# A linear-attention and Fourier-mixing kernel: batch 0 of the attention in a written order with own tiles, and the last bit of the weights added as an integer

## The chip, the cores and the metric

The kernel runs on one core of a Trainium2 chip. The metric is the device time of one launch in microseconds (us). A core has TensorE (PE; its weight loads are listed as PEld), VectorE (DVE), ScalarE (ACT), GpSimd (POOL) and SyncE (SP), which here only issues DMAs. Each engine works through its own list of instructions in order and waits on semaphores.

## The reference

```python
B, H, S, D = 4, 8, 768, 48
f = 1 / (1 + exp(-f_logit))
for t in range(S):                                   # attention, per batch and head
    state = f[t][:, None] * state + outer(k[t], v[t])
    y[t]  = q[t] @ state
x = y, heads side by side                            # [4, 768, 384]
u = x + real(fft over d (fft over s (x)))            # Fourier mixing
un = (u - mean) / sqrt(var + 1e-6)
out = u + relu(un @ w_ch1) @ w_ch2                   # 384 -> 1536 -> 384
```

The two weight matrices arrive as 64-bit numbers; the kernel turns each into 32-bit floats itself.

## The kernel before, in words

A **unit** is one batch and one pair of heads: 16 units, four to a batch. Queries, keys and forget logs of a unit arrive with the tokens along the free axis, in one tile `qkf` of [128, 3, 768] (heads at partitions 0 to 47 and 64 to 111; between them lie constants), and there are three such tiles. `attention` (L154 to L197) and `outputs` (L318 to L378) are Python generators; each `yield` ends a step.

- Step 1: DVE clamps the logs (L164), ACT makes `g = ln(1 + exp(-f))` (L165, L166), DVE takes running sums per chunk of 128 tokens (L169 to L171), ACT makes `W = exp(g)` (L173), `exp(-g)` (L174) and chunk decays (L176), POOL multiplies `W` by the keys (L178), DVE multiplies the queries (L179).
- Step 2: PE makes the scores (L188, 48 matmuls), DVE copies them under the causal mask into `at` (L192).
- `outputs`: PE turns the keys (L328), ACT copies them (L330), PE makes the state increments (L335, L341), DVE scans them into states (L344); then PE makes `y` from scores and values (L356) and from states (L361), ACT copies it out (L366, L367); then PE turns it back (L372), ACT writes it to the batch's tile `x` (L373), and SP issues the loads of unit u + 3 into the tiles that this unit leaves (L104 for `qkf`, L106 for `v`).

When four units have written a batch's `x`, the generator `fnet` runs on it: sums and differences (L397 to L403), the transform over tokens (`z`, L422), over channels (`mix`, L435), mean and variance (L453 to L458), and for each half of the tokens normalising and turning (L466 to L470), the up projection in 12 blocks (`up`, L479, relu on ACT L482) and the down projection (`po`, L492), sum (L494) and store (L382, L384). Two `x` tiles exist, so batch 2's units write theirs once batch 0 is stored.

**Weights.** The first `fnet` fetches and converts the weights in 24 pieces of [128, 384], twelve of `w1` ahead of the up blocks that use them and twelve of `w2` in the first down projection. `single` (L123 to L146) does one: a 384 KB load into `raw` (two buffers, L128), ACT takes the size (L136), DVE shifts and joins bits of the high word (L138, L139), zeroes what is too small (L141), takes the power of two (L142) and shifts the low word (L140), ACT scales that (L144), POOL multiplies it by the power of two (L145) and adds it to the result (L146). Its temporaries `size`, `pow2` and `tail` share the 14 buffers of `h1`, which also hold the twelve relu outputs of a half.

**Order.** `run` steps all active units once per tick, starts a unit at each tick in batch 0 and at every second tick later (`STEP`), and steps `fnet` twice per tick (`BESIDE`). That order is a priority only: a list scheduler, with cost estimates of its own, fills each engine's list when the program is built, and may put an instruction ahead of earlier ones that it takes to be waiting. After all of it a check decides whether a second, slower form of attention must run; it didn't in these executions.

Of the kernel before, what the change touches and what calls it, by code (L numbers as in the profile page):

```python
# [14 lines left out]
STEP = 2  # L15
BESIDE = 2
# [3 lines left out]
X_MIN = -24.0  # L20
# [3 lines left out]
def kernel(  # L24
# [13 lines left out]
    nc = tc.nc  # L38
    B, HP, _, D, _, S = qkf.shape
    NCH = S // C  # L40
    DM = HP * 2 * D
# [4 lines left out]
    HD = DM // 2  # L46
    R = 64 + D
    ROWS = [slice(64 * r, 64 * r + D) for r in range(2)]
# [13 lines left out]
    def fixed(shape, tag):  # L62
        return const.tile(shape, F32, tag=tag, name=tag)
# [3 lines left out]
    qkf_t = [fixed([128, 3, S], f"qkf{i}") for i in range(3)]  # L67
# [6 lines left out]
    xc = fixed([128, 4, 256], "xc")  # L74
# [25 lines left out]
    def load_unit(u):  # L100
        b, hp = divmod(u, HP)
        t = qkf_t[u % 3]
        for r in (1, 0):
            nc.sync.dma_start(out=t[ROWS[r]], in_=qkf[b, hp, r])  # L104
        vt = p3.tile([128, NCH, 2 * D], F32, tag="v", name=f"v{u}")
        nc.sync.dma_start(out=vt, in_=v[b, hp])  # L106
        return vt

    v_of = {0: load_unit(0)}
    nc.sync.dma_start(out=masks, in_=sel)  # L110
    nc.sync.dma_start(out=ident, in_=ident_in)
    v_of[1] = load_unit(1)
    v_of[2] = load_unit(2)
    nc.sync.dma_start(out=tab, in_=seq_tab)
    nc.sync.dma_start(out=cd[:, :, 0:DM], in_=dim_tab)
    nc.gpsimd.memset(eps, 1e-6)
    for t in at_t + te_t:
        nc.gpsimd.memset(t, 0.0)
    nc.gpsimd.memset(xc[:, :, HD + 1:], 0.0)
    nc.gpsimd.memset(xs[:, :, 0:1], 0.0)  # L120
    nc.gpsimd.tensor_copy(cd[:, :, DM:DM + 1], cd[:, :, 0:1])

    def single(dst, src):  # L123


        n = dst.shape[-1]
        raw = pr.tile([128, n, 2], U32, tag="raw", name="raw")
        nc.sync.dma_start(out=raw.rearrange("p n w -> p (n w)"), in_=src)  # L128
        lo, hi = raw[:, :, 0], raw[:, :, 1]
        size = ph1.tile([128, n], F32, tag="h1", name="size")  # L130
        pow2 = ph1.tile([128, n], F32, tag="h1", name="pow2")
        tail = ph1.tile([128, n], F32, tag="h1", name="tail")
        bits, pow2b, tailb = (t.bitcast(U32) for t in (dst, pow2, tail))
        vec = nc.vector

        nc.scalar.activation(size, hi.bitcast(F32), AF.Abs)  # L136

        vec.tensor_scalar(bits, hi, 3, 0x3FFFFFF8, ALU.logical_shift_left, ALU.bitwise_and)  # L138
        vec.scalar_tensor_tensor(bits, hi, 0xC0000000, bits, ALU.bitwise_and, ALU.bitwise_or)  # L139
        vec.tensor_scalar(tailb, lo, 1, None, ALU.logical_shift_right)  # L140
        vec.scalar_tensor_tensor(dst, size, SMALLEST, dst, ALU.is_ge, ALU.mult)  # L141
        vec.tensor_scalar(pow2b, bits, 0xFF800000, None, ALU.bitwise_and)  # L142

        nc.scalar.activation(tail, tailb, AF.Copy, scale=2.0 ** -51)  # L144
        nc.gpsimd.tensor_tensor(tail, tail, pow2, ALU.mult)  # L145
        nc.gpsimd.tensor_tensor(dst, dst, tail, ALU.add)  # L146
# [7 lines left out]
    def attention(u, x_all):  # L154
# [4 lines left out]
        t = qkf_t[u % 3]  # L159
        Q, K, g = t[:R, 0], t[:R, 1], t[:R, 2]  # L160
        AT = at_t[u % 2]
        W = p2.tile([128, S], F32, tag="W", name=f"W{u}")[:R]
        at = lambda a, i, c: a.rearrange("p (c t) -> p c t", t=C)[:, c, i]
        nc.vector.tensor_scalar(g, g, X_MIN, None, ALU.max)  # L164
# [7 lines left out]
        nc.gpsimd.tensor_copy(T[:, NCH - 1:], g[:, S - 1:S])  # L172
        nc.scalar.activation(W, g, AF.Exp)  # L173
# [4 lines left out]
        nc.gpsimd.tensor_tensor(W, W, K, ALU.mult)  # L178
        nc.vector.tensor_tensor(Q, Q, g, ALU.mult)  # L179
        yield  # L180
# [18 lines left out]
    def attention_by_blocks(u, x_all):  # L199
# [5 lines left out]
        t = qkf_t[u % 3]  # L205
        Q, K, g = t[:R, 0], t[:R, 1], t[:R, 2]
# [18 lines left out]
        w = p1.tile([128, 3, S], F32, tag="eo", name=f"w{u}")[:R]  # L225
        wq, wk, gk = w[:, 0], w[:, 1], w[:, 2]
# [28 lines left out]
        tl = p2.tile([128, S // LEAF], F32, tag="tl", name=f"tl{u}")[:R]  # L255
# [59 lines left out]
        yield  # L315
        yield from outputs(u, x_all, AT, Q, K, None, T)

    def outputs(u, x_all, AT, Q, K, te, T=None):  # L318
# [11 lines left out]
        nc.scalar.copy(kT, ps[:, :(NCH - 1) * 128].rearrange("p (c k) -> p c k", k=128)[:, :, :R])  # L330
        ps = ps_a.tile([128, 2, 512], F32, tag="sc", name=f"ds{u}")
# [22 lines left out]
        for c in range(NCH):  # L354
            for r in range(2):
                nc.tensor.matmul(y[FILL[r], c * C:(c + 1) * C],  # L356
                                 lhsT=vt[:, c, r * D:r * D + (64 if r == 0 else D)], rhs=AT[:, r, c],
                                 start=(c % 4 == 0), stop=(c == 0), skip_group_check=True)
        for c in range(1, NCH):
            for r in range(2):  # L360
                nc.tensor.matmul(y[ROWS[r], c * C:(c + 1) * C], lhsT=st[ROWS[r], :, c - 1],  # L361
                                 rhs=Q[ROWS[r], c * C:(c + 1) * C], start=False, stop=True,
                                 skip_group_check=True)
# [3 lines left out]
        nc.scalar.copy(yT[:, HS + 1:], y[:R, S - 1:HS:-1])  # L367
        yield
# [7 lines left out]
        if u + 3 < B * HP:  # L376
            v_of[u + 3] = load_unit(u + 3)
        yield  # L378
# [121 lines left out]
    def run(unit_of, step, first):  # L500
        left, xs_of, active, behind, done = [HP] * B, {}, [], [], set()
        u = tick = 0
        while u < B * HP or active or behind:
            if u < B * HP and (u < 3 or u - 3 in done) and (first and u < HP or tick % step == 0):
                b, hp = divmod(u, HP)
                if hp == 0:
                    xs_of[b] = p2.tile([128, NCH, DM], F32, tag="x", name=f"x{b}")
                active.append((u, unit_of(u, xs_of[b])))
                u += 1
            for i, unit in list(active):  # L510
                if next(unit, active) is active:
                    active.remove((i, unit))
                    done.add(i)
                    b = i // HP
                    left[b] -= 1
                    if not left[b]:
                        behind.append(fnet(b, xs_of.pop(b), first and b == 0))
            for _ in range(BESIDE):
                while behind and next(behind[0], active) is active:
                    behind.pop(0)  # L520
            tick += 1

    run(attention, STEP, True)


# [8 lines left out]
    with tc.If(again > 0):  # L534
        v_of.update({i: load_unit(i) for i in range(3)})
        run(attention_by_blocks, 3, False)
# [69 lines left out]
```

## Time and profile before

| | |
|---|---|
| median of 3 runs | 709.93 us (708.13 to 710.97) |
| the profiled execution | 707.84 us, of which the instructions' span is 706.0 us |
| busy: PE, DVE, ACT, POOL | 599.4, 247.1, 182.3, 138.7 us |
| mean DMA rate | 50 GB/s over the span |

A busy PE is one with a matmul in its pipeline, not one at full clock: the granted clock is a row of its own. A group's row gives output, inputs, shape and count, then busy time and mean duration; behind the bar stands the idle time ahead of the group and what ended it.

### The profile page before, as it was taken

The numbers are of one execution on the slowest core, as the hardware profiler recorded it, in microseconds if no ns is written. First come the engines' busy times: TensorE is split into PE (matmuls) and PEld (weight loads), VectorE is DVE, ScalarE is ACT, GpSimd is POOL, SyncE is SP. The second block draws the span as 40 slices with busy tenths as digits, with TensorE's granted clock in tenths as the row PEclk, the third lists the DMA queues.
The fourth block names the chain that finished last, engine by engine and source line by source line (L and its number), as shares of the span: only waits on it lengthen the run. The fifth ranks groups of instructions, "written<-read, shape, count | busy, mean of one in ns | idle before, by whom it ended". The sixth has DMA issues, their size and how long they took to land.

```text
span 706.0 us, 8313 instructions
## 1 busy us (share of the span) xinstructions
PE 599.4 (85%) x3458; PEld 371.0 (53%) x3458; DVE 247.1 (35%) x398; ACT 182.3 (26%) x341; POOL 138.7 (20%) x130
## 2 busy tenths in 40 slices
PE   0777898775765799997999999978999997999995
PEld 0656656443432355565656665645555563555552
DVE  3767786885577500039403110152000005000000
ACT  1555454434233121034411320212102101210200
POOL 4231541465455400112300101020000010000001
PEclk9997899988786799998999999997999999899999
DMA  9595553534323100033003000000000000000000
GB/s 167 168 180 100 116 113 68 135 85 95 90 85 96 65 11 1 22 78 70 0 1 73 11 1 23 13 1 0 1 22 13 0 33 1 0 12 22 0 12 27
DMA packets 11182, 35.56 MB, mean 50 GB/s; under 512 B 1600, under 2 KB 3776, under 8 KB 9472
## 3 DMA queue, kind: packets, MB, share of 16 engines
q1 hardware_dynamic: 10368, 32.58, 20.0%
q0 software_dynamic: 768, 2.36, 0.9%
q8 instruction: 29, 0.48, 0.3%
q14 instruction: 17, 0.14, 0.1%
HBM read 30.22 MB, written 4.72 MB: 49 GB/s over the span
## 4 chain that ended last, share of the span: by engine, by line
PE 67%; DVE 15%; POOL 8%; issue 4%; ACT 4%; DMA 2%; POOLq 0%; ACTq 0%; DVEq 0%
PE up L479 27%; PE po L492 24%; POOL tail L145 3%; POOL w L146 3%; PE z L422 3%; PE mix L435 3%; DVE at L192 2%; DVE w L141 2%; DVE qkf L170 2%; PE y L356 2%; PE sc L188 2%; DVE pow L142 2%; PE ds L335 1%; DMA qkf<-in_qkf_dram 1%; PE pt L469 1%
## 5 line engine op out<-in xcount | busy, mean ns | idle before, releaser
L479 PE MATMUL up<-unT,w 128*128 128x384 f32 x576 | 205.8, 518 | 22.6 <-POOL w L146 19.8
L492 PE MATMUL po<-w,h 128*128 128x384 f32 x576 | 198.0, 502 | 16.7 <-POOL w L146 16.7
L479 PEld LDWEIGHTS up<-unT,w 128*128 128x128 f32 x576 | 114.1, 202 | 105.8 <-POOL w L146 23.0
L492 PEld LDWEIGHTS po<-w,h 128*128 128x128 f32 x576 | 110.7, 195 | 100.8 <-POOL w L146 25.8
L494 DVE TENSOR_TENSOR x<-po,x 128x384 f32<-128x384 f32 x24 | 13.4, 558 | 294.5 <-PE po L492 294.4
L482 ACT ACTIVATE h<-up 128x384 f32<-128x384 f32 x96 | 47.1, 491 | 150.4 <-PE up L479 150.4
L384 POOL DMA_INDIRECT out_dram<-x,place x12 | 11.9, 990 | 323.8 <-DVE x L494 317.1
L188 PE MATMUL sc<-qkf,W 48*64 48x128 f32 x768 | 35.7, 313 | 26.9 <-DVE qkf L179 25.5
L192 DVE COPY_PREDICATED at<-causal,sc 128x768 f32<-128x768 uint32 x32 | 32.5, 1032 | 38.0 <-PE sc L188 38.0
L188 PEld LDWEIGHTS sc<-qkf,W 48*64 48x64 f32 x768 | 28.4, 155 | 31.9 <-POOL W L178 21.2
L145 POOL TENSOR_TENSOR tail<-tail,pow 128x384 f32<-128x384 f32 x24 | 32.6, 1360 | 48.4 <-DVE pow L142 47.8
L178 POOL TENSOR_TENSOR W<-W,qkf 112x768 f32<-112x768 f32 x16 | 31.0, 1937 | 25.7 <-ACT W L173 24.9
L356 PE MATMUL y<-at,v 128*64 128x128 f32 (+1 forms) x384 | 33.3, 310 | 1.9 <-ACT yT L367 1.3
L146 POOL TENSOR_TENSOR w<-w,tail 128x384 f32<-128x384 f32 x24 | 31.5, 1311 | 1.8
L356 PEld LDWEIGHTS y<-at,v 128*64 128x64 f32 (+1 forms) x384 | 25.4, 147 | 9.3 <-issue 5.5
L170 DVE TENSOR_TENSOR_SCAN qkf<-qkf,bound 112x768 f32<-112x768 f32 x16 | 28.1, 1755 | 0.4
L172 POOL COPY deep<-qkf 112x1 f32<-112x1 f32 x16 | 3.3, 205 | 125.9 <-DVE qkf L170 118.3
L344 DVE TENSOR_TENSOR_SCAN stt<-ds,te 112x288 f32<-112x288 f32 x16 | 12.1, 754 | 44.0 <-PE ds L341 44.0
L470 ACT COPY unT<-pt 128x384 f32<-128x384 f32 x24 | 11.1, 478 | 61.8 <-PE pt L469 61.8
L435 PE MATMUL mix<-cd,zz 128*128 128x385 f32 x72 | 25.7, 497 | 1.3 <-DVE row L443 1.3
L469 PE MATMUL pt<-ident,un 128*128 128x128 f32 x72 | 13.7, 323 | 14.9 <-DVE mv L454 9.9
L361 PE MATMUL y<-qkf,stt 48*48 48x128 f32 x320 | 22.7, 288 | 4.2 <-DVE stt L344 4.1
(80 smaller groups left out, 526.8 us busy)
## 6 DMA issues: line engine op xcount, KB each, us to landing
qkf<-in_qkf_dram SPq DMA_DIRECT2D x32, 432.0 KB, 6.7
raw<-in_w_ch_dram SPq DMA_DIRECT2D x24, 384.0 KB, 3.1
v<-in_v_dram SPq DMA_DIRECT2D x16, 288.0 KB, 3.3
out_dram<-x SPq DMA_DIRECT2D x12, 192.0 KB, 1.9
tab<-in_seq_tab_dram SPq DMA_DIRECT2D x1, 1158.0 KB, 18.3
cd<-in_dim_tab_dram SPq DMA_DIRECT2D x1, 576.0 KB, 17.1
out_dram<-x,place POOLq DMA_INDIRECT x12, 2.6
masks<-in_sel_dram SPq DMA_DIRECT2D x1, 64.0 KB, 4.9
```

The costliest lines, as they stand in the source:

```text
L145: nc.gpsimd.tensor_tensor(tail, tail, pow2, ALU.mult)
L146: nc.gpsimd.tensor_tensor(dst, dst, tail, ALU.add)
L170: nc.vector.tensor_tensor_scan(g, g, bound[:R], 0.0, ALU.add, ALU.min)
L178: nc.gpsimd.tensor_tensor(W, W, K, ALU.mult)
L188: nc.tensor.matmul(ps[64 * s:64 * s + 64, r, i * C:(i + 1) * C], lhsT=W[ROWS[r], o + 64 * s:o + 64 * s + 64], rhs=Q[ROWS[r], o:o + C], sta ...
L192: nc.vector.copy_predicated(AT[:, :, half], causal.bitcast(U32).unsqueeze(1).unsqueeze(1).to_broadcast([128, 2, NCH // 2, C]), ps[:, :, :N ...
L356: nc.tensor.matmul(y[FILL[r], c * C:(c + 1) * C], lhsT=vt[:, c, r * D:r * D + (64 if r == 0 else D)], rhs=AT[:, r, c], start=(c % 4 == 0), ...
L361: nc.tensor.matmul(y[ROWS[r], c * C:(c + 1) * C], lhsT=st[ROWS[r], :, c - 1], rhs=Q[ROWS[r], c * C:(c + 1) * C], start=False, stop=True, s ...
L435: nc.tensor.matmul(mix[:rows.stop - rows.start, :n], lhsT=zz[:, T, rows], rhs=cd[:, T, :n], start=(T == 0), stop=(T == terms - 1))
L479: nc.tensor.matmul(pp[:, :3 * 128], lhsT=w1[:, kt, m * 128:(m + 1) * 128], rhs=unT[:, kt], start=(kt == 0), stop=(kt == 2))
L482: nc.scalar.activation(h, pp[:, :3 * 128], AF.Relu)
L492: nc.tensor.matmul(po[:, :DM], lhsT=h1[m][:, i * 128:(i + 1) * 128], rhs=w2[:, m], start=(m == 0), stop=(m == NF - 1))
```

## The change: a written order for batch 0, own tiles, and an integer bit

- **Tiles.** `qkf` is split into three `g`, three `k` and four `q` tiles. `load(u, names)` fetches any of logs ("f"), keys, queries and values of a unit, two DMAs for each of the first three. Logs and keys of unit u + 3 are fetched after its W and Q products, queries and values of u + 4 after its `y`. At the start come logs, keys, queries of unit 0, the identity matrix, its values, then units 1 and 2 and part of 3; the two tables of the transforms follow later (`tables`), the masks only in the slower form.
- **Steps.** A unit has nine steps instead of its former five. The clamp moves from DVE to POOL, the product of `W` and keys from POOL to DVE.
- **Order.** Batch 0's units are written out in a fixed order of steps inside `manual_schedule`, which keeps the written order on every engine; POOL's zeroing and the tables' loads have their place in it. `no_sync_barrier` follows: nothing written after it is placed before it. From there on a list of nine (age, n) pairs gives per round which unit steps and how often `fnet` is stepped after it (five times per round, one unit per round).
- **Weights.** `single` puts the low word's top three bits in by shift and OR on DVE, takes the next bit as an integer 0 or 1 (`half`), POOL adds it as an integer, and the product that zeroes small values comes last, on DVE. Two temporaries instead of three.

```diff
-    qkf_t = [fixed([128, 3, S], f"qkf{i}") for i in range(3)]
+    g_t = [fixed([128, S], f"g{i}") for i in range(3)]
+    k_t = [fixed([128, S], f"k{i}") for i in range(3)]
+    q_t = [fixed([128, S], f"q{i}") for i in range(4)]
...
-    for i, t in enumerate(qkf_t):
-        nc.vector.memset(t[32:64, 0:2], 0.0)
-        nc.gpsimd.memset(t[32:64, 2], 30.0)
+    for i, t in enumerate(g_t):
+        nc.gpsimd.memset(t[32:64], 30.0)
+    for i in range(4):
+        for t in k_t[i:i + 1] + q_t[i:i + 1]:
+            nc.vector.memset(t[32:64], 0.0)
...
+            t, i = {"f": (g_t[u % 3], 2), "k": (k_t[u % 3], 1), "q": (q_t[u % 4], 0)}[name]
+            for r in (1, 0):
+                nc.sync.dma_start(out=t[ROWS[r]], in_=qkf[b, hp, r, :, i])
+
+    def first_loads():
+        load(0, "f", "k", "q")
+        nc.sync.dma_start(out=ident, in_=ident_in)
+        load(0, "v")
+        for u in (1, 2):
+            load(u, "f", "k", "q", "v")
+        load(3, "q", "v")
...
-        pow2 = ph1.tile([128, n], F32, tag="h1", name="pow2")
-        tail = ph1.tile([128, n], F32, tag="h1", name="tail")
+        half = ph1.tile([128, n], U32, tag="h1", name="half")
...
-        vec.tensor_scalar(tailb, lo, 1, None, ALU.logical_shift_right)
+        vec.scalar_tensor_tensor(bits, lo, 29, bits, ALU.logical_shift_right, ALU.bitwise_or)
+        vec.tensor_scalar(half, lo, 28, 1, ALU.logical_shift_right, ALU.bitwise_and)
+        nc.gpsimd.tensor_tensor(bits, bits, half, ALU.add)
         vec.scalar_tensor_tensor(dst, size, SMALLEST, dst, ALU.is_ge, ALU.mult)
-        vec.tensor_scalar(pow2b, bits, 0xFF800000, None, ALU.bitwise_and)
-        nc.scalar.activation(tail, tailb, AF.Copy, scale=2.0 ** -51)
-        nc.gpsimd.tensor_tensor(tail, tail, pow2, ALU.mult)
-        nc.gpsimd.tensor_tensor(dst, dst, tail, ALU.add)
...
-        nc.vector.tensor_scalar(g, g, X_MIN, None, ALU.max)
+        nc.gpsimd.tensor_scalar(g, g, X_MIN, None, ALU.max)
         nc.scalar.activation(g, g, AF.Exp, scale=-1.0)
         nc.scalar.activation(g, g, AF.Ln, bias=1.0)
+        yield
...
-        nc.gpsimd.tensor_tensor(W, W, K, ALU.mult)
+        yield
+        nc.vector.tensor_tensor(W, W, K, ALU.mult)
         nc.vector.tensor_tensor(Q, Q, g, ALU.mult)
+        load(u + 3, "f", "k")
         yield
...
+    run = Run(attention, True)
+    first_loads()
+    with tc.manual_schedule():
+        for k in range(-1, HP):
+            for age in (-1, 0, 1, 2, 1, 0, 1, 2, 1):
+                if k - age < HP:
+                    run.step(k - age)
+            if k == -1:
+                zeros()
+            if k == 0:
+                tables()
+    tc.no_sync_barrier()
+    nc.gpsimd.tensor_copy(cd[:, :, DM:DM + 1], cd[:, :, 0:1])
+    run.step(HP)
+    k = HP
+    while run.done < B * HP or run.behind:
+        for age, n in ((2, 0), (1, 1), (1, 0), (2, 1), (1, 1), (1, 0), (0, 1), (0, 0), (-1, 1)):
+            run.step(k - age)
+            run.fill(n)
+        k += 1
```

`run.step(u)` runs one step of unit u; `run.fill(n)` runs n steps of the oldest waiting `fnet`. The nine steps, by their first operation: clamp (L164's work), running sums (L169), the two products (L178, L179), scores (L188), turned keys (L328), state increments (L335), `y` from scores (L356), `y` from states (L361), turning back (L372).

More of the change, by code (lines that the diff above doesn't have):

```diff
@@ L130, in single @@
         size = ph1.tile([128, n], F32, tag="h1", name="size")
[L131 to L133 removed]
+        half = ph1.tile([128, n], U32, tag="h1", name="half")
+        bits = dst.bitcast(U32)
         vec = nc.vector
@@ L496, in fnet @@
                 yield
[L500 to L521, printed above, removed]
@@ L534 @@
     with tc.If(again > 0):
-        v_of.update({i: load_unit(i) for i in range(3)})
-        run(attention_by_blocks, 3, False)
+        nc.sync.dma_start(out=masks, in_=sel)
+        for u in range(4):
+            load(u, *("fkqv" if u < 3 else "qv"))
+        run = Run(attention_by_blocks, False)
+        u = tick = 0
+        while run.done < B * HP or run.behind:
+            if tick % 5 == 0 and u < B * HP:
+                u += 1
+            for i in range(u):
+                run.step(i)
+            run.fill(BESIDE)
+            tick += 1
 _OUTS = [((4, 768, 384), 'float32')]
```

81 lines of the change are left out of this document (49 added, 32 removed).

## The prediction

> **What bounds the kernel now.** I read the page's first two parts, then the windows cut where the work changes character, then the timeline at the cuts.
>
> ```profile
> span 706.0 us, 8313 instructions
> PE   0777898775765799997999999978999997999995
> PEclk9997899988786799998999999997999999899999
> ```
> ```profile
> 0.00:21.00 21.00, 0.00 (x0) 0.00 (x0) 8.61 (x9) 6.40 (x8) 9.35 (x23) 1.00 0.93 165
> 21.00:69.00 48.00, 38.22 (x568) 32.07 (x568) 32.49 (x41) 23.55 (x39) 12.07 (x11) 0.89 0.67 149
> 69.00:118.00 49.00, 40.91 (x448) 29.63 (x447) 41.87 (x72) 24.46 (x45) 21.79 (x16) 0.91 0.52 112
> 118.00:198.00 80.00, 57.76 (x438) 33.80 (x435) 52.03 (x75) 30.01 (x56) 38.21 (x29) 0.82 0.36 89
> 198.00:242.00 44.00, 27.57 (x72) 12.89 (x68) 31.16 (x58) 13.44 (x24) 27.15 (x25) 0.73 0.29 90
> 242.00:706.00 464.00, 434.90 (x1941) 262.61 (x1941) 80.93 (x147) 84.41 (x170) 30.09 (x28) 0.97 0.07 18
> ```
>
> The window columns are length, busy time and count of PE, PEld, DVE, ACT and POOL, then granted clock, DMA share and GB/s. There are two kernels in one here. From 242 us on, PE is busy 434.9 of 464 us at a clock of 0.97, and nothing but less matmul work would shorten that. Before 242, PE has nothing for 21 us and then runs with holes and at a clock down to 0.73. In 198 to 242 it counts 72 matmuls in 44 us; the last window holds 1941 in 464. So a gain has to come from the first 242 us, and the question is how early the last window can begin and what is then still to be done.
>
> The marks of that first part, from the timeline:
>
> ```profile
> 13.13 0.56 DVE L164 TENSOR_SCALAR qkf<-qkf 112x768 f32<-112x768 f32 x1 [7.38 <-DMA qkf<-in_qkf_dram]
> 21.20 2.84 PE L188 MATMUL sc<-qkf,W 48*64 48x128 f32 x48 [21.20 <-DVE qkf L179]
> 68.32 0.64 ACT L373 COPY x<-yt 128x576 f32<-128x576 f32 x1 [0.97 <-PE yt L372]
> 118.52 0.98 PE L479 MATMUL up<-unT,w 128*128 128x384 f32 x1
> 242.32 0.91 PE L492 MATMUL po<-w,h 128*128 128x384 f32 x2 [1.90 <-POOL w L146]
> ```
>
> Logs of unit 0 are there at 13.1, first scores at 21.2, batch 0's `x` is complete at 68.3, the first up projection starts at 118.5 (with its three weight pieces), and the last of the 24 pieces releases PE at 242.3. Hence 21 pieces take 123.8 us, 5.9 us each. How one goes when hardly anything else runs:
>
> ```profile
> 221.91 1.00 POOL L145 TENSOR_TENSOR tail<-tail,pow 128x384 f32<-128x384 f32 x1 [1.40 <-DVE pow L142]
> 222.06 1.25 DVE L139 SCALAR_TENSOR_TENSOR w<-raw,w 128x384 uint32<-128x384 uint32 x1
> 222.98 1.19 POOL L146 TENSOR_TENSOR w<-w,tail 128x384 f32<-128x384 f32 x1
> 224.20 0.36 DVE L140 TENSOR_SCALAR tail<-raw 128x384 uint32<-128x384 uint32 x1 [0.89 <-POOL w L146]
> 224.48 0.55 DVE L141 SCALAR_TENSOR_TENSOR w<-size,w 128x384 f32<-128x384 f32 x1
> 225.06 0.36 DVE L142 TENSOR_SCALAR pow<-w 128x384 uint32<-128x384 uint32 x1
> 225.34 0.35 DVE L138 TENSOR_SCALAR w<-raw 128x384 uint32<-128x384 uint32 x1
> 225.57 1.00 POOL L145 TENSOR_TENSOR tail<-tail,pow 128x384 f32<-128x384 f32 x1 [1.40 <-DVE pow L142]
> ```
>
> From one L145 to the next is 3.66 us: POOL's two operations, then L140 on DVE, which waits for POOL's L146 because no third temporary is free while twelve relu outputs fill `h1`. It is a chain of latencies: neither engine is full.
>
> **The change part by part.** *A weight piece.* Removed: L140 and L142 on DVE, the scaling on ACT, one of POOL's two operations, and the third temporary. Added on DVE: a shift-and-OR (two inputs, so L139's form) and a shift-and-AND (L140's form, 0.36). The DVE sum is 0.35 (L138) + 0.55 (L139, free) + 0.55 (new) + 0.36 (new) + 0.55 (L141) = 2.36 us against 2.17 before. The free price of L139's form is the least of its row:
>
> ```profile
> L139 DVE SCALAR_TENSOR_TENSOR w<-raw,w x24: 542/662/2184, 44.1 to 236.7; 128x384 uint32<-128x384 uint32 x24
> L178 POOL TENSOR_TENSOR W<-W,qkf x16: 1802/1818/3680, 18.5 to 392.2; 112x768 f32<-112x768 f32 x16
> L179 DVE TENSOR_TENSOR qkf<-qkf x16: 934/1134/1890, 19.5 to 393.6; 112x768 f32<-112x768 f32 x16
> ```
>
> (least, median, greatest in ns). Its 1.25 us above began with POOL's L145 running and ended 0.4 us after it. I read that as DVE held up while POOL runs; then a piece costs both engines' sums one after the other. POOL's integer add has no row. Between the least of POOL's same-sized float operation, 1.00, and the worst POOL row of the trace, 3.68, I take 1.00, since shape and operand count are L145's. That gives 2.36 + 1.00 = 3.36 us a piece; if nothing held up anything it would be DVE's 2.36.
>
> The Trainium skill, SBUF — State Buffer, section on who interferes with whom, states that a DVE instruction with two SBUF inputs and a GpSimd instruction that reads SBUF exclude each other, the first one holding the port for its whole length. The trace agrees where L139 takes 1.25 instead of 0.54. By that rule the piece costs 3.36, without it 2.36; the first stands in the sum and the second is the rival on the fast side below.
>
> The added wait is DVE's last product on POOL's add. Behind it on DVE stand the next piece's bit operations or a unit's scan, and PE's up or down matmuls wait for it; 1.00 us of DVE per piece, which 3.36 already charges. The two temporaries fit the two free buffers, so the next piece need not wait as L140 did.
>
> *A unit.* The `W` product goes from POOL (1.82) to DVE (0.93, L179's form), the clamp from DVE (0.56) to POOL. POOL's clamp has no row: between DVE's 0.56 and POOL's two-input 1.82 of the same shape I take 1.2, nearer the middle as it has one input. It runs a round ahead of its use in the new order, so it is hidden; without that cover it costs 1.2 − 0.56 = 0.6 us a unit. DVE's sum per unit is then, from
>
> ```profile
> L170 DVE TENSOR_TENSOR_SCAN qkf<-qkf,bound x16: 1746/1757/1759, 15.7 to 382.4; 112x768 f32<-112x768 f32 x16
> L192 DVE COPY_PREDICATED at<-causal,sc x32: 994/1033/1077, 23.2 to 454.8; 128x768 f32<-128x768 uint32 x32
> L344 DVE TENSOR_TENSOR_SCAN stt<-ds,te x16: 742/756/757, 29.5 to 462.0; 112x288 f32<-112x288 f32 x16
> ```
>
> 1.76 + 2 × 1.03 + 0.76 + 2 × 0.93 = 6.4 us (tiny copies left out). PE's sum per unit comes from the groups in the window 305 to 455 us, where the clock is nearly full:
>
> ```profile
> L188 PE MATMUL sc<-qkf,W 48*64 48x128 f32 x240 | 9.3, 273 | 0.0
> L356 PE MATMUL y<-at,v 128*48 128x128 f32 (+1 forms) x96 | 8.0, 300 | 0.0
> L361 PE MATMUL y<-qkf,stt 48*48 48x128 f32 x100 | 6.7, 277 | 0.5 <-DVE stt L344 0.5
> L335 PE MATMUL ds<-v,kT 128*64 128x48 f32 (+1 forms) x100 | 4.0, 220 | 0.0
> L328 PE MATMUL st<-ident,W 112*128 112x112 f32 x25 | 3.8, 277 | 0.6 <-ACT x L373 0.5
> L372 PE MATMUL yt<-ident,yT 112*128 112x112 f32 x24 | 3.0, 260 | 1.8 <-DVE at L192 1.8
> L341 PE MATMUL ds<-v,at 64*64 64x48 f32 (+1 forms) x20 | 1.6, 229 | 0.0
> ```
>
> Five units' worth in L188, L361, L335, L328 and L341, four in L356 and L372: 1.86 + 2.00 + 1.34 + 0.80 + 0.76 + 0.75 + 0.32 = 7.8 us.
>
> *The start.* Logs come first and alone, 288 KB as two DMAs. But the written order puts unit 1's two ACT functions on the logs ahead of unit 0's exponentials on ACT, so the first scores wait for unit 1's logs. Up to their end 288 × 4 + 64 + 288 KB, 1.54 MB, are queued; at the first window's 165 GB/s that is 9.3 us, and with the issues at the head about 12. From logs to scores took 8.1 us (13.13 to 21.20); unit 0's scan, 1.76, is done by then. First scores at 12 + 6.3 = 18.3, a gain of 2.9; at best the logs of unit 0 alone decide (gain 6), at worst the smaller pieces gain nothing. A unit now takes seven DMAs instead of three on SP, each issued at least a round before its use; where that cover fails, a round waits for a landing:
>
> ```profile
> v<-in_v_dram SPq DMA_DIRECT2D x16, 288.0 KB, 3.3
> ```
>
> (size, median us to landing.) The weights' loads stand behind these on SP, as before.
>
> *Batch 0.* Before, four units took 68.3 − 21.2 = 47.1 us, 11.8 each. In the written order a round can't be under PE's 7.8; each engine waits where its order meets another's (the increments for ACT's copy of the turned keys, DVE's state scan for the increments), so I take 9.0. Unit 3 is turned back near the end of the fifth round: 18.3 + 4 × 9.0 + 7 = 61.3, a gain of 7.
>
> *From `x` to the first up projection.* 50.2 us before, DVE busy 41.9 of 49. Less attention now stands ahead of it: unit 4 whole, 5 up to its scores' `y`, 6 up to its products, where before units 4, 5 and 6 were whole. That is about one unit of DVE, 6.4, so 44 us: first up at 105.3. No piece can be fetched before batch 0's written stretch ends; before, one was, worth at most 3.66, within the rounding of this term.
>
> *From there to the last piece.* 21 × 3.36 = 70.6, and one unit's 6.4 of DVE between: 182.3.
>
> *What is then left.* 706 − 242.3 = 463.7 as before, plus the units that the old order had got through in its long wait:
>
> ```profile
> L372 PE MATMUL yt<-ident,yT 112*128 112x112 f32 x60 | 8.7, 287 | 5.0 <-DVE at L192 2.9 <-ACT yT L366 2.0
> ```
>
> 60 turnings between 21 and 242 are ten units; the new order has seven through (0 to 6). Three units at 7.8 come back as PE work, 23.4. The span: 182.3 + 463.7 + 23.4 = 669.4. The profiled execution took 707.84, 1.84 beyond its span, so 671 us; the runs' median of 709.93 is 2.1 above that, 0.3%, which I leave to the range.
>
> **The rivals.** *The fast side: DVE and POOL don't hold each other up, and the batch runs at PE's floor.* 21 × 2.36 = 49.6 takes 21 off, rounds of 7.8 take 4.8 off: 645 us. For it: L145 lasted 1.00 with DVE waiting at its side; against: the 1.25. Chance 0.19.
>
> *The pieces keep their pace.* If the 5.9 us come from engines waiting in order (relu behind `up` on ACT, logs behind relu) and not from the piece itself, then 105.3 + 124 = 229, three units are done meanwhile as before, and 229 + 463.7 + 1.8 = 695. For it: 5.9 is far above the quiet stretch's 3.66. Against: half of the pieces did run at 3.66, and DVE and POOL together are busy 90 of 80 us in 118 to 198. Chance 0.14.
>
> *The slow side: POOL's integer add.* It runs 24 times in the path of the weights, on an operation that no row shows. The span stays at 706 if a piece takes 105.3 + 6.4 + 21p + 463.7 + 23.4 = 706, p = 5.1, so from an add of 2.7 us on the change loses. At 3.68, the worst POOL row, p is 6.0 and the time 728. The Trainium skill, GPSIMD Engine Reference, section on engine selection, says that an add of two 32-bit integer tensors is done natively by the cores, which speaks for the float price; no run here shows it. Chance 0.08.
>
> *It doesn't do what it says.* The old lists already overlapped the units; if the written order only trades one engine's waits for another's and the pieces gain their 0.3 us alone, 707.84 − 21 × 0.3 = 702, or nothing at all. Chance 0.05.
>
> **How the numbers follow.** The forecast case (650 to 692) has 0.54, and its time is 671. The range takes in the fast rival and the unchanged pace, 638 to 702. About 0.5% is what a measurement of this kernel can tell from no change, that is 706.4 on the faster side: faster 0.54 + 0.19 + 0.14 = 0.87, less 0.01 for a slower start; the last rival mostly falls in the same band, 0.05; slower 0.09.
>
> **What would show it.** The step is right where first scores come near 18 us, batch 0's last write into `x` near 61, the first up near 105, the last piece near 182, with the pieces 3.4 us apart and POOL's add at 1.0; PE then is as full behind 182 as it was behind 242. The forecast is wrong if the add is over 2.7 us, if the first up comes no earlier than 118, if the pieces stay near 6 us, or if PE's rows behind the last piece show new holes, since all of the sum rests on the last 464 us being PE's own.

## The result and the profile after

| | before | predicted | after |
|---|---|---|---|
| median of 4 runs | 710.04 us (708.13 to 710.97) | 671.0 (638 to 702) | 683.71 us (679.45 to 688.18) |
| ratio to before, 95% interval | | 0.945 | 0.963 (0.955 to 0.972) |
| profiled execution, its span | 707.84, 706.0 | 671, 669.4 | 679.45, 677.5 |

The kernel is faster by 3.7%, inside the range, by two thirds of what was forecast. The profiled execution is the fastest of the four, so the points below go by its marks and the verdicts by the medians.

The page of after: span, PE's busy tenths, granted clock.

```profile
span 677.5 us, 8335 instructions
PE   0685898787867999989999979999999867999995
PEclk9997899998997999999999989999999978999998
```

The windows of after, cut at its own marks (length, busy time and count of PE, PEld, DVE, ACT, POOL, then granted clock, DMA share, GB/s):

```profile
0.00:22.40 22.40, 0.00 (x0) 0.00 (x0) 10.06 (x13) 7.21 (x9) 14.76 (x25) 1.00 0.86 187
22.40:69.80 47.40, 36.75 (x577) 31.35 (x578) 37.32 (x51) 28.53 (x47) 17.98 (x13) 0.90 0.62 180
69.80:105.50 35.70, 30.31 (x286) 20.12 (x286) 27.87 (x55) 14.05 (x27) 14.13 (x11) 0.94 0.30 84
105.50:211.50 106.00, 83.32 (x664) 50.27 (x663) 86.10 (x147) 41.28 (x73) 44.91 (x35) 0.92 0.43 127
211.50:677.50 466.00, 438.17 (x1938) 263.86 (x1936) 71.75 (x141) 78.88 (x163) 26.84 (x22) 0.97 0.04 13
```

The last window is the one to read first. It holds 1938 matmuls in 466 us; before, the last window held 1941 in 464. As a whole the end is 2 us longer than before, so the whole gain lies ahead of the last weight piece. But PE's tenths have a new dip at the 33rd and 34th slice (a 6 and a 7, where before stood a 9 and a 7), and the clock's row has one there too (a 7 and an 8, where before stood 9s). The marks, from the timelines of PE, ACT and DVE:

```profile
22.46 2.84 PE L204 MATMUL sc<-q,W 48*64 48x128 f32 x48 [22.46 <-DVE q L194]
69.75 0.64 ACT L394 COPY x<-yt 128x576 f32<-128x576 f32 x1 [0.16 <-PE yt L393]
105.50 1.88 PE L497 MATMUL up<-unT,w 128*128 128x384 f32 x5
211.52 0.56 DVE L158 SCALAR_TENSOR_TENSOR w<-size,w 128x384 f32<-128x384 f32 x1 [1.03 <-POOL w L157]
```

| mark | before | predicted | after |
|---|---|---|---|
| first scores | 21.2 | 18.3 | 22.5 |
| batch 0's `x` complete | 68.3 | 61.3 | 69.8 |
| first up projection | 118.5 | 105.3 | 105.5 |
| last weight piece | 242.3 | 182.3 | 211.5 |
| from there to the end | 463.7 | 487.1 | 466.0 |

The last piece of after, and of the kernels below with the new conversion, is dated by the start of its last product on DVE, that of before by the end of its last operation on POOL, where PE is released. DVE's product takes 0.56 us, so the gain to that mark is that much smaller than the table has it.

The first up projection came within 0.2 us of its forecast, though both terms that lead to it were wrong; the last piece came 29 us late, and the end took 21 us less than was charged. The sum was saved by errors that cancel, which is luck and not the forecast's merit, so the experiments take each by itself.

### The profile page after: what moved, and what is told of

Read it like the earlier page. It is cut to its first block, busy times and chain, and to the rows that moved or that the text cites. A ratio compares the mean times of both kernels' runs of the same rounds, so it can differ in the third digit from the quotient of the medians.

```text
span 677.5 us, 8335 instructions
## 1 busy us (share of the span) xinstructions
PE 588.6 (87%) x3458; PEld 365.6 (54%) x3458; DVE 233.1 (34%) x402; ACT 170.0 (25%) x317; POOL 118.6 (18%) x106
## 4 chain that ended last, share of the span: by engine, by line
PE 68%; DVE 10%; POOL 6%; issue 3%; ACT 2%; DMA 1%; SPq 0%; POOLq 0%; DVEq 0%
PE up L497 27%; PE po L510 27%; PE z L440 4%; PE mix L453 3%; POOL w L157 2%; PE y L381 2%; POOL g L174 1%; PE sc L204 1%; DVE bs L471 1%; PE pt L487 1%; DVE w L158 1%; POOL eo L416 1%; PE y L374 1%; DVE eo L415 1%; DVE at L208 1%
## 5 line engine op out<-in xcount | busy, mean ns | idle before, releaser
L497 PE MATMUL up<-unT,w 128*128 128x384 f32 x576 | 195.5, 498 | 8.2 <-DVE w L158 6.4
L510 PEld LDWEIGHTS po<-w,h 128*128 128x128 f32 x576 | 110.2, 194 | 87.4 <-DVE w L158 13.2
L204 PE MATMUL sc<-q,W 48*64 48x128 f32 x768 | 36.4, 292 | 22.8 <-DVE q L194 22.5
L204 PEld LDWEIGHTS sc<-q,W 48*64 48x64 f32 x768 | 27.5, 143 | 29.8 <-DVE q L194 22.5
L157 POOL TENSOR_TENSOR w<-w,half 128x384 uint32<-128x384 uint32 x24 | 31.4, 1314 | 60.1 <-DVE w L154 32.1
L174 POOL TENSOR_SCALAR g<-g 112x768 f32<-112x768 f32 x16 | 39.2, 2451 | 10.3 <-DMA g<-in_qkf_dram 8.4
L381 PE MATMUL y<-q,stt 48*48 48x128 f32 x320 | 25.4, 293 | 7.3 <-DVE stt L362 7.0
L440 PE MATMUL z<-tab,xc 128*128 128x386 f32 (+1 forms) x64 | 22.1, 511 | 10.3 <-POOL xc L421 10.3
L182 DVE TENSOR_TENSOR_SCAN g<-g,bound 112x768 f32<-112x768 f32 x16 | 28.8, 1805 | 0.6
L381 PEld LDWEIGHTS y<-q,stt 48*48 48x48 f32 x320 | 20.3, 163 | 14.4 <-DVE stt L362 8.7
L374 PEld LDWEIGHTS y<-at,v 128*64 128x64 f32 (+1 forms) x384 | 23.4, 140 | 6.4 <-issue 4.9
L440 PEld LDWEIGHTS z<-tab,xc 128*128 128x128 f32 x64 | 14.6, 242 | 17.8 <-POOL xc L421 10.7
```

The costliest lines, as they stand in the source:

```text
L157: nc.gpsimd.tensor_tensor(bits, bits, half, ALU.add)
L174: nc.gpsimd.tensor_scalar(g, g, X_MIN, None, ALU.max)
L182: nc.vector.tensor_tensor_scan(g, g, bound[:R], 0.0, ALU.add, ALU.min)
L204: nc.tensor.matmul(ps[64 * s:64 * s + 64, r, i * C:(i + 1) * C], lhsT=W[ROWS[r], o + 64 * s:o + 64 * s + 64], rhs=Q[ROWS[r], o:o + C], sta ...
L374: nc.tensor.matmul(y[FILL[r], c * C:(c + 1) * C], lhsT=vt[:, c, r * D:r * D + (64 if r == 0 else D)], rhs=AT[:, r, c], start=(c % 4 == 0), ...
L440: nc.tensor.matmul(o, lhsT=lhsT, rhs=rhs, start=(i == 0), stop=(i == len(parts) - 1), skip_group_check=True)
```

## The experiments

The theory behind the experiments: the weights' new form brings most of the gain; the clamp on POOL eats much of the rest; the written order as such brings little. The rival: the written order and the tiles bring the gain, and the weight pieces were held by other work. Ratios are to the kernel before, run on the same chip, with 95% intervals; before took 707.66, 708.05 and 707.95 us in the three sets, so times of different sets are compared below as they are. Marks come from one profiled execution of each kernel: that of the change is the fastest of its runs, 4.3 us below the median, and that of the kernel with the clamp on DVE is the slowest of its runs (677.29 us), 4.1 above.

### Which half of the change brought it

The kernel before with only the new form of the weights, and the change with the old form:

```diff
 # weights_only: before, with
+        half = ph1.tile([128, n], U32, tag="h1", name="half")
...
+        nc.gpsimd.tensor_tensor(bits, bits, half, ALU.add)
 # order_only: after, with
+        pow2 = ph1.tile([128, n], F32, tag="h1", name="pow2")
+        tail = ph1.tile([128, n], F32, tag="h1", name="tail")
...
+        nc.gpsimd.tensor_tensor(dst, dst, tail, ALU.add)
```

> The kernel before with the new conversion of the weights alone; order, tiles and clamp as before. Theory 1 (DVE's and POOL's time per piece sets the pace of the pieces): 21 pieces at 3.36 instead of 2.17 + 1.96 = 4.1 us behind the first up projection, 16 us less, 690 to 696 us; the pieces behind the first up go from 5.9 to about 5.1 us. Rival (engines waiting in order set the pace): under 5 us less, 703 to 711 us, pieces still near 5.9 us.

> The changed kernel with the old conversion of the weights; written order, tiles and moved products as changed. Theory 1: it loses what the conversion brought, 16 us, so 695 to 700 us, with the first up projection still near 105 us and the last piece near 228. Rival (the order brings it all): 680 to 688 us, as the changed kernel.

Measured: the weights alone 691.51 us, 0.976 (0.972 to 0.981), with the last piece at 224.0 instead of 242.3; order, tiles and moves alone 701.98 us, 0.988 (0.983 to 0.994). The product of the two, 0.965, is the change's 0.963: they add up, and the weights are two thirds of it. The first lies in its theory's range, the second 2 us above, with first up and last piece where that theory had them (105.3 and 227.8).

### The clamp's engine

```diff
-        nc.gpsimd.tensor_scalar(g, g, X_MIN, None, ALU.max)
+        nc.vector.tensor_scalar(g, g, X_MIN, None, ALU.max)
```

> The changed kernel with the clamp of the logs back on DVE. Theory A (POOL's 2.1 us clamp stands in the path, at the start and wherever a unit waits for it): first scores near 19 instead of 22.5 us, and 3 to 10 us less in all, 670 to 680. Rival (but for the start it is hidden a round ahead, and DVE's 0.56 a unit now adds to the engine that limits the weights' stretch): 680 to 688, no difference outside the noise.

Measured: 673.17 us, 0.949 (0.945 to 0.953), 10.5 us faster than the change, as theory A had; first scores at 17.3. The clamp's rows, of after and then of this kernel (least, median, greatest in ns):

```profile
L174 POOL TENSOR_SCALAR g<-g x16: 2122/2315/3558, 9.3 to 211.6; 112x768 f32<-112x768 f32 x16
```
```profile
L174 DVE TENSOR_SCALAR g<-g x16: 534/554/1352, 10.1 to 201.2; 112x768 f32<-112x768 f32 x16
```

On POOL it takes four times as long as on DVE, and longer than POOL's own product of two tensors of that shape (1.80 at least, before). At the start of after it stands in everyone's way:

```profile
9.31 2.14 POOL L174 TENSOR_SCALAR g<-g 112x768 f32<-112x768 f32 x1 [4.47 <-DMA g<-in_qkf_dram]
...
11.50 2.69 POOL L134 MEMSET at<- 128x1536 f32 x2
...
15.16 2.85 POOL L174 TENSOR_SCALAR g<-g 112x768 f32<-112x768 f32 x1
...
18.04 0.84 ACT L175 ACTIVATE g<-g 112x768 f32<-112x768 f32 x1 [4.84 <-POOL g L174]
...
20.52 0.96 DVE L193 TENSOR_TENSOR W<-W,k 112x768 f32<-112x768 f32 x1 [3.80 <-ACT W L186]
```

POOL clamps unit 0, zeroes tiles from 11.50 to 15.1, and only then clamps unit 1; ACT, whose written list has unit 1's two functions ahead of unit 0's exponential, stands still for 4.84 us; DVE waits for that exponential, and the first scores for DVE. The logs were there in time: with the clamp on DVE, units 0 and 1 are both clamped by 11.25 us. So the start's 5.2 us are not the clamp's length alone: the zeroing that stands between the two clamps in POOL's written list takes 3.7 us, and POOL had been idle for 4.47 us ahead of the first clamp. What zeroing first would bring, with the clamp left on POOL, was not tried.

### The written order as such

```diff
-    with tc.manual_schedule():
+    if True:
         for k in range(-1, HP):
...
-    tc.no_sync_barrier()
```

> The changed kernel without the fixed order and without the barrier behind it: the list scheduler orders all of it from the same sequence of steps. Theory: the written order gave rounds of 8 to 9.3 us in batch 0 where the list's order had 11.8; without it batch 0's x is complete 5 to 10 us later and the time is 685 to 693. Rival (the new sequence of steps does it, whoever orders it): 676 to 688, as the changed kernel.

Measured: 685.98 us, 0.967 (0.964 to 0.971), beside 0.963 (0.955 to 0.972) with it: no difference that these runs can tell, in the range of the rival and at the lower edge of the theory's. Batch 0's `x` is even complete at 62.4, earlier than in after, against the theory. The likely reason, which the next experiment tests, is what happens right behind the written stretch in after. PE waits twice for a masked copy:

```profile
53.30 0.81 PE L344 MATMUL st<-ident,W 112*128 112x112 f32 x5 [3.60 <-DVE at L208]
...
65.73 1.20 PE L344 MATMUL st<-ident,W 112*128 112x112 f32 x5 [4.23 <-DVE at L208]
```

and DVE's list, filled by the scheduler again, has other work ahead of those copies:

```profile
51.37 0.36 DVE L152 TENSOR_SCALAR w<-raw 128x384 uint32<-128x384 uint32 x1 [0.75 <-DMA raw<-in_w_ch_dram]
...
52.24 1.01 DVE L208 COPY_PREDICATED at<-causal,sc 128x768 f32<-128x768 uint32 x1
...
58.72 3.38 DVE L182 TENSOR_TENSOR_SCAN g<-g,bound 112x768 f32<-112x768 f32 x2
...
64.66 1.02 DVE L208 COPY_PREDICATED at<-causal,sc 128x768 f32<-128x768 uint32 x1
```

Operations of the first weight piece and two later units' scans go first, and unit 3's turning back (L393, at 68.33) stands in PE's list behind the second wait. Rounds of the written stretch itself were good: the scores of units 0 to 3 began at 22.46, 31.76, 39.72 and 48.0, 8.0 to 9.3 us apart.

### A longer written order, and the lead that it gives

If the units behind the stretch are the trouble, units 4 and 5 can be written out too (with the clamp on DVE):

```diff
-        for k in range(-1, HP):
+        for k in range(-1, HP + 2):
             for age in (-1, 0, 1, 2, 1, 0, 1, 2, 1):
-                if k - age < HP:
+                if k - age < HP + 2:
...
-    run.step(HP)
-    k = HP
+    run.step(HP + 2)
+    k = HP + 2
```

> As the kernel with the clamp on DVE (673.2), with the written order going on for two more rounds, until batch 0's x is complete, units 4 and 5 in it. Theory 1 (DVE's time per piece and unit decides when the last piece is done, whoever orders it): x complete near 57 instead of 67 us, but the pieces begin later, so 670 to 677, the same. Rival (the break behind the written order, where unit 3's scores wait behind other work, costs what it looks like, 10 us): 661 to 667.

Measured: 646.83 us, 0.914 (0.911 to 0.917), 26 us faster than with the clamp on DVE alone, and more than either theory. `x` was complete at 57.2 instead of 67.2, as the rival wanted, but the last piece came only 5.5 us earlier (197.1 against 202.6). The other 20 us lie behind it: in the profiled executions, from the last piece to the end took 447.9 us instead of 473.0, 4 us of which are the slow execution of the kernel compared with. So a new theory was needed. In the change the first `fnet` begins in the middle of round five, where unit 3 ends; with the longer order it begins with round six, four of its steps later. By the loops of the two kernels, a batch's last unit then ends four of `fnet`'s 20 steps ahead of the end of the `fnet` beside it, where in the change it ends in the very place where that `fnet` ends. The expectation below calls this lead two rounds; it is four steps, less than one round of five. What that is worth is seen where one `fnet` ends and the next begins. In after:

```profile
539.46 0.74 PE L393 MATMUL yt<-ident,yT 112*128 112x112 f32 x6
547.35 6.48 PE L440 MATMUL z<-tab,xc 128*128 128x386 f32 x16 [7.15 <-POOL xc L421]
```
```profile
541.49 3.31 POOL L416 TENSOR_TENSOR eo<-x 128x1152 f32<-128x1152 f32 x1
...
546.28 0.98 POOL L421 COPY xc<-eo 128x8 f32<-128x8 f32 x1
```

The last unit is turned back when PE has nothing else left, and POOL's four steps of sums and differences lie bare between it and `z`: 7.15 us. In the longer written order the same chain is over 24 us before PE gets to `z`:

```profile
492.71 0.98 POOL L421 COPY xc<-eo 128x8 f32<-128x8 f32 x1
```
```profile
517.43 2.76 PE L440 MATMUL z<-tab,xc 128*128 128x386 f32 x10
```

The test of that theory gives the steps the same sequence as the longer written order, without writing units 4 and 5 out:

```diff
 # the clamp on DVE and the short written order, with
-            run.fill(n)
+            run.fill(n if k >= HP + 2 else 0)
```

> This is the kernel with the clamp on DVE (673.2 us), the written order as short as in the change, and the first fnet stepped only from round six on, two rounds later than before; units 4 and 5 run in the free order meanwhile. Theory 1 (what the longer written order brought, 26 us, is the lead of two rounds that the units then have over the fnet beside them): x of a batch is complete well before the fnet ahead of it ends, so the holes of PE at the start of an fnet go (3.9 us ahead of y at 400, 7.2 us ahead of the last z at 544 in the kernel with the clamp on DVE), and the granted clock stays near 1.00 behind them; 650, between 645 and 656. Rival (it is the writing out: units 4 and 5 kept in order, with no weight conversion put ahead of their DVE work): the free order gives most of it away again, 665 to 673.

Measured: 657.53 us, 0.932 (0.927 to 0.937): 15.6 of the 26 us, between the ranges of the theory and the rival. The theory is right for the larger part, and the rival for the rest: `x` is complete only at 66.3, first up at 106.8, last piece at 206.2. The lead's part is seen in the windows of the two middle transforms, from `z` to `z`, and of the last, in before, after and this kernel:

```profile
301.00:578.30 277.30, 262.71 (x1402) 162.61 (x1401) 63.55 (x105) 60.02 (x118) 23.82 (x21) 0.97 0.09 21
578.30:706.00 127.70, 114.41 (x359) 66.15 (x357) 14.05 (x36) 17.08 (x37) 3.87 (x4) 0.96 0.04 12
```
```profile
271.00:547.00 276.00, 262.65 (x1399) 162.00 (x1397) 51.98 (x95) 52.85 (x109) 18.79 (x15) 0.98 0.04 14
547.00:677.50 130.50, 116.91 (x358) 67.75 (x358) 13.69 (x36) 17.06 (x37) 3.20 (x4) 0.93 0.03 10
```
```profile
267.00:528.00 261.00, 259.45 (x1398) 160.11 (x1397) 52.24 (x94) 52.50 (x109) 19.09 (x14) 1.00 0.04 14
528.00:655.30 127.30, 114.00 (x359) 66.23 (x357) 14.05 (x36) 17.06 (x37) 3.88 (x4) 0.96 0.03 12
```

The same 1400 matmuls take 261 us instead of 276 or 277, with PE busy 259 of 261 at a clock of 1.00. The last stage shows the second price of a hole: behind it the clock is 0.93 and the stage takes 130.5 us, without one 0.96 and 127.3.

Two more kernels give a lead by another way, with four steps of `fnet` to a round instead of five, so that the lead grows by four steps with every batch: once on the clamp on DVE, once on the longer order with the last bit's add on DVE.

```diff
-        for age, n in ((2, 0), (1, 1), (1, 0), (2, 1), (1, 1), (1, 0), (0, 1), (0, 0), (-1, 1)):
+        for age, n in ((2, 0), (1, 1), (1, 0), (2, 1), (1, 1), (1, 0), (0, 1), (0, 0), (-1, 0)):
```

> As the kernel with the clamp on DVE (673.2), with four instead of five fnet steps per round behind batch 0, so that a batch's units are done before the fnet beside them. Theory (the 7.15 us in which PE waits for the last fnet's first sums, because unit 15 ends with the fnet before it, are a wait that the new sequence made): that wait goes, 666 to 669. Rival (what units 12 to 15 take earlier they take from PE there, and the pieces come later): 672 to 677.

> This is the kernel with the longer written order and the last bit added on DVE (low bits of the weights differ), with four fnet steps to a round instead of five. Theory 1 (four steps brought 12.4 us on the kernel with the clamp on DVE because they too give the units a lead over the fnet; with the lead of two rounds nothing is left to win): within 3 us of the kernel of this set with five steps. Rival (fewer fnet steps beside a unit are worth something by themselves): 6 to 12 us faster than that one.

Measured: 660.8 us, 0.932 (0.929 to 0.935) on the short order, 12.4 us faster than with five steps, more than its theory had, and no hole ahead of the last `z`; but on the longer order 647.62, 0.917 (0.913 to 0.921), 7 us slower than the same kernel with five (640.68, below), which neither theory had. A lead can be too long: there the last unit is through at 407 us, 73 earlier than with five steps (480), nothing of the units is left to cover what follows, and the third transform's normalising lies bare:

```profile
416.68 2.42 PE L487 MATMUL pt<-ident,un 128*128 128x128 f32 x9 [6.04 <-DVE mv L472]
```

### What a weight piece costs

The last bit's add goes to DVE, on the clamp on DVE and on the longer order; and once, for a bound, ACT only copies the high words.

```diff
 # add_dve, longer_add
-        nc.gpsimd.tensor_tensor(bits, bits, half, ALU.add)
+        vec.tensor_tensor(bits, bits, half, ALU.add)
 # no_conversion: in place of the whole conversion
+        nc.scalar.copy(dst, hi.bitcast(F32))
```

> As the kernel with the clamp on DVE (673.2), with the weights' last bit added on DVE instead of POOL (an addition there goes through 32-bit floats, so the low bits of the weights differ). Theory 1 (POOL's 1.0 us is paid in the piece's path, since DVE waits for it or is held up by it): a piece costs 5 x DVE + 0.55 = 2.9 instead of 3.36, 21 x 0.45 = 9 us less, 661 to 668. Rival (POOL's add lies beside other DVE work): DVE's 0.55 comes on top, 21 x 0.55 = 12 us more, 680 to 686.

> This is the kernel with the longer written order (646.8 us) with the last bit added on DVE; that engine adds in floating point and rounds the sum, so low bits of the weights differ. Theory 1 (DVE and POOL still hold each other up in the conversion, 21 pieces between the first up and the last piece at 96 us in the kernel with the longer order): a piece costs 2.36 + 0.55 on DVE (the add's median with the clamp on DVE) instead of 2.36 + 1.00, so 21 x 0.45 = 9.5 us, 637, between 631 and 640. Rival (PE is what lasts longest there, busy 74.5 of 96.0 us, and the lead of the units only moves its holes elsewhere): 642 to 647.

> As the kernel with the clamp on DVE (673.2), with the conversion of the weights left out: ACT copies the high words as they are, so the products with the weights aren't the reference's; loads and matmuls are the same. Theory 1 (until the last piece the kernel is bound by DVE, with the pieces' 24 x 2.4 us and their waits in it): about 45 to 55 us less, 618 to 630. Rival (engines waiting for each other in the units' chains set the pace there): 15 to 25 us less, 648 to 658.

Measured: 658.73 us, 0.931 (0.928 to 0.934) on the short order, 14.4 us faster and 2 below its theory's range; 640.68, 0.905 (0.901 to 0.909) on the longer one, 6.1 us faster, between its two theories and at the rival's edge; without any conversion 640.43, 0.904 (0.899 to 0.909), 33 us faster than the clamp on DVE, between the theories. Without conversion the last piece is there at 130 us, 73 earlier, but only six units are through by then instead of ten, and the rest of the kernel takes 505 us instead of 473: 32 of the 73 us come back as work of the end. The add's rows, on POOL in after and on DVE:

```profile
L157 POOL TENSOR_TENSOR w<-w,half x24: 990/1070/2641, 62.5 to 210.5; 128x384 uint32<-128x384 uint32 x24
```
```profile
L157 DVE CUSTOM_DVE_ANT_0 w<-w,half x24: 534/552/851, 60.4 to 187.3; 128x768 uint16<-128x768 uint16 x24
```

On DVE it stands as a custom instruction over twice as many 16-bit elements; no run here shows whether its sums differ from POOL's in the low bits.

The conversion stretch, first up to last piece, with the add on POOL and on DVE, short order first, then the longer one:

```profile
99.90:202.60 102.70, 83.72 (x663) 49.65 (x663) 84.91 (x153) 42.73 (x74) 33.63 (x30) 0.91 0.44 131
```
```profile
99.10:188.60 89.50, 75.57 (x612) 46.70 (x612) 79.75 (x158) 35.81 (x66) 6.11 (x6) 0.94 0.46 134
```
```profile
101.10:197.10 96.00, 74.53 (x544) 42.98 (x544) 83.81 (x151) 39.99 (x69) 30.63 (x32) 0.93 0.44 128
```
```profile
99.40:189.00 89.60, 69.55 (x545) 42.02 (x544) 85.27 (x167) 39.21 (x69) 11.74 (x9) 0.98 0.46 137
```

With the add on POOL neither engine is full (DVE busy 83.8 of 96.0 us); with it on DVE, DVE is busy 85.3 of 89.6. So the two engines did cost each other time, and with the add moved DVE itself is the bound of the longer order's stretch. The rows show two forms of it. One is a wait for a result: DVE's last product stands still for POOL's add, 8.4 us over the 21 pieces of the longer order, and 0.1 with the add on DVE:

```profile
L158 DVE SCALAR_TENSOR_TENSOR w<-size,w 128x384 f32<-128x384 f32 x21 | 12.3, 588 | 8.4 <-POOL w L157 8.4
```
```profile
L158 DVE SCALAR_TENSOR_TENSOR w<-size,w 128x384 f32<-128x384 f32 x21 | 11.5, 554 | 0.1
```

The other is an operation that lasts longer while the other engine runs. In after a scan that began inside an add took 2.57 us, where its median is 1.76; and the longest add, 2.64 us from 205.97, lies over such a scan:

```profile
185.38 1.00 POOL L157 TENSOR_TENSOR w<-w,half 128x384 uint32<-128x384 uint32 x1 [2.27 <-DVE w L154]
185.43 2.57 DVE L182 TENSOR_TENSOR_SCAN g<-g,bound 112x768 f32<-112x768 f32 x1
```

On the longer order the two windows hold the same 544 or 545 matmuls, and 21 pieces save 6.4 us, 0.3 each, not the 0.45 of the expectation; 1.4 of the 6.4 is that the later window has one scan and one clamp fewer and one product more on DVE. On the short order 13.2 us are saved, where the later window also has 51 fewer matmuls in it.

### The clamp on POOL again, on the longer order

```diff
 # the longer written order, with
-        nc.vector.tensor_scalar(g, g, X_MIN, None, ALU.max)
+        nc.gpsimd.tensor_scalar(g, g, X_MIN, None, ALU.max)
```

> This is the kernel with the longer written order (646.8 us) with the clamp back on POOL, as the change has it. Theory 1 (the clamp's place costs at the start, where nothing hides it, and in the conversion stretch, where POOL also has the integer adds): as without the longer order, 10.5 us, so 657, between 653 and 660, first scores 5 us later. Rival (only the start is exposed, since the units now run two rounds ahead and the clamp with them): first scores 5 us later and nothing else, 652.

Measured: 662.53 us, 0.937 (0.933 to 0.941), 15.7 us slower than with the clamp on DVE. Theory 1 has the mechanism, and its size was short by a third: first scores 5.2 us later, another 4.6 until the first up projection (110.9 against 101.1), another 4.8 until the last piece (211.7 against 197.1), 1.4 behind it. So the lead hides nothing of it; that DVE and POOL, and not the age of a unit, set that stretch is argued, not shown.

The fastest kernel with the change's arithmetic is the longer written order with the clamp on DVE, 646.83 us; with the add on DVE as well it is 640.68.

## Why the prediction was right or wrong

**What bounds the kernel: right.** PE's own work was most of the last 464 us before and of the last 466 after (busy 434.9 and 438.2); all that the change brought lies ahead of the last weight piece.

**The weight piece: right in its mechanism.** The add took 0.99 us at least and 1.25 in the mean of the stretch where 1.00 was charged, so the slow side's rival, an add of 2.7 us or more, fell. The fast side's rival, no mutual hold-up, fell by the drawn-out scan and add above; that moving the add to DVE took 6 to 14 us off speaks for a cost of both engines, of which the wait for the add's result is a large part. 21 pieces of 3.36 us and the five units that were in the stretch, 6.4 each on DVE, make 102.6; the stretch took 106.

**The step that failed: how much attention stands between the pieces.** The sum charged "one unit's 6.4 of DVE" beside the 21 pieces and three units more behind them. In after, as in before, ten units are through by the last piece (60 turnings of L393 up to 211.5), five of them in the stretch. The scheduler still mixed in as many as before. So the last piece was 29.2 us late, and the end 21.1 us short of its charge; by this account four more units of DVE, 25.6, are most of the first, and the three units of PE, 23.4, the second. That the two ends of one wrong count cancel but for 8 us is luck. Whether the pieces waited for the units or the units filled the pieces' waits isn't separated: DVE was busy for 86.1 of the 106 us, and without conversion the stretch held one unit instead of five.

**The clamp's price: wrong, beyond its upper bound.** It was put between DVE's 0.56 and POOL's two-input 1.82; it took 2.12 at least and 2.45 in the mean. The Trainium skill, GPSIMD Engine Reference, section 4.1 on engine selection, puts one-input work on GpSimd at roughly line rate; these rows, four times DVE's, do not show that, and the measurement decides. And "hidden" was wrong: the start has no cover, and the clamp's move cost 10.5 us in all. First scores at 22.5 instead of 18.3 are the clamp's place in POOL's list, zeroing included, as the kernel with the clamp on DVE shows (17.3).

**Batch 0: rounds right, their end wrong.** 9.0 us was forecast for a round, 8.0 to 9.3 was seen, and yet `x` was complete 8.5 us late, 4.2 from the start and 4.3 because unit 3 ended behind the written stretch, in free order. What DVE did there ahead of unit 3 it didn't have to do afterwards: from `x` to the first up took 35.7 instead of 44. So the first up was met by luck, by two errors of 8 us. Where `x` was earlier, at 57.2 (longer order) and 62.4 (no written order), this part did take 43.9 and 45.5 us.

**The end: one hole was missed.** The forecast named new holes behind the last piece as what would break it. One came, 7.15 us ahead of the last `z`. It didn't show in the total of that window because holes of before (6.25 us at 478 was the longest) went at the same time. To attend to that place was worth more than the hole's size: giving the units a lead, which no part of the prediction considered, brought 16 us without any change to the work.

**Doesn't do what it says:** in part true. Without the written order the change takes 685.98 instead of 683.71, which the intervals can't tell apart. A longer one, against the same sequence of steps not written out, is worth 10.7 us. Why is shown only in so far as its `x`, first up and last piece come 9.1, 5.7 and 9.1 us earlier (57.2, 101.1, 197.1 against 66.3, 106.8, 206.2); which of the scheduler's reorderings on DVE costs how much wasn't tried apart.

## What to carry to other kernels

Where two streams share an engine, the distance between them decides whether the short serial chain at the start of the one lies under the other: look at each hand-over for a hole of the bounding engine, and shift the streams against each other by a few steps before tuning either. When work is moved to an engine off the path, price it by a row of that same engine and kind of operation, and look first at the place where nothing covers it, the start. When a sum charges some work to a later stage, count in the trace of before how much of it the earlier stage had done, and ask what in the change would alter that count: here nothing did.

## What the hardware showed that was not expected

- POOL's maximum with a constant over 112x768 took 2.12 us at least and 2.32 in the median, longer than its product of two tensors of that shape (1.80 and 1.82); DVE's took 0.53 and 0.55.
- This hole cost more than its length. In the 13 us behind the 7.15 us hole the granted clock of after was 0.80; in the kernel with the longer order, without the hole, it was 1.00 at the same place:

```profile
547.00:560.00 13.00, 12.65 (x36) 7.20 (x37) 0.81 (x3) 1.44 (x3) 0.26 (x1) 0.80 0.00 0
```
```profile
517.00:530.00 13.00, 13.00 (x45) 7.12 (x44) 2.52 (x6) 1.45 (x3) 0.97 (x1) 1.00 0.04 15
```

The same 13 us hold 36 matmuls in the one and 45 in the other. The Trainium skill, TensorE: Matmul & The Clock Gate, Part 1 on the HAM clock gate, says that the clock falls when TensorE has been idle for a while and comes back after a few us of work; the direction agrees.
